# Moving the splits behind a normalisation, and additions, statistics and turns one step on, in a state-space and MLP kernel

## The chip, the core and the metric

The kernel runs on one core of a Trainium2 chip. The metric is device time in microseconds (us) of one execution; before the change it is 699.3 us, the median of three runs (698.97 to 700.25). The core has a matrix engine (TensorE, PE in the profile, with its weight loads as PEld), a vector engine (VectorE, DVE), an activation engine (ScalarE, ACT), a general engine (GpSimd, POOL) and a queue that issues DMAs (SyncE, SP). Each engine works through its own list of instructions strictly in the order written; semaphores join the lists.

## What is computed

Two residual blocks on x of 2048 rows (time) by 512 columns (channels), all in float32:

```python
def _A_ref(u, ...):                       # S4D convolution along time
    K = 2.0 * jnp.einsum("dn,dnl->dl", C, P).real
    y = irfft(rfft(u_t, 2 * L) * rfft(K, 2 * L))[:, :, :L]
    return y + u * D_skip
def _B_ref(x, w1, w2, w3, w4):
    h = _gelu(_layernorm(x) @ w1)
    hs = concat(h shifted by +1, -1, +2, -2 rows, one quarter of the channels each) @ w2
    x1 = x + hs
    return x1 + _gelu(_layernorm(x1) @ w3) @ w4
h  = x + _A_ref(_layernorm(x), ...)
h2 = h + _B_ref(_layernorm(h), w1, w2, w3, w4)
```

w3 is 512 by 1792, w4 is 1792 by 512.

## The kernel before

The convolution (`conv_phase`) takes the first 303 us and is not touched. A planner writes its order; after it, everything in `mixer_phase` runs in the order in which the Python code stands. Whatever one function issues to an engine stands in that engine's list behind what earlier calls issued.

**Tiles and groups.** The 2048 rows of h are 16 tiles of 128 rows, tile j in `h[:, j, :]`; four tiles make a group, so group q holds tiles 4q to 4q+3. Every matrix product is made of three float32r products (high by high, high by low, low by high), so each factor is split into a high half (a rounding copy) and a low half (the difference). Matmuls of the mixer are 128x128 by 128x512.

**Layers 1 and 2.** `layer1(q, f)` makes 12 matmuls and a GELU. `layer2(j)` (line 1265) makes 12 matmuls for tile j into one of four rotating PSUM banks and lets VectorE write x1 of the tile from it; in the profile these blocks are `l`, and their evacuation is `xq<-h,rr,l`. For tiles 0 to 7 it calls at once `residual(j)`, which adds x1 to h (on GpSimd for tiles below 12, on VectorE from 12 on; `h<-h,xq`), and `stats2(j)`, two VectorE instructions for mean and variance (`st`, `mv`).

**The second normalisation.** `norm2_ops(q)` (line 1290) gives, for a whole group, eleven small VectorE steps on 128x4 numbers that work out 1/sqrt(var) and the offset (`qa`, `qb`, `qr`, `qo`), and then four normalisations of 128x512, on ScalarE; of group 1 the last is VectorE's. `norm2(q)` issues all of them at once.

**Turns.** The normalised groups have to be transposed. `turn2(q)` (line 1314) does it with four VectorE block transposes and 16 DMAs within the core's memory, in SP's queue; `turn2_wide(1)` with 16 TensorE transposes into four wide banks (`x1t`), each bank copied out by ScalarE.

**Layer 3 with seven products.** The product with w3 uses Strassen's scheme (in Winograd's form) on pairs of groups: pair 0 is groups 0 and 1, pair 1 groups 2 and 3. Its left factors are the turned blocks b11, b21, b22 and the sums t1 to t4 from `sums2` (four VectorE subtractions for each half c), each split by `halve` (line 1340): the high half on ScalarE, the low half on VectorE, or on GpSimd where told. For pair 0, b11 and b21 (turned group 0) are split on GpSimd (`b1100l` to `b2101l`), before `layer2(7)`.

**The loop of steps** (line 1542) runs s = 0 to 13; steps 0 to 6 work on pair 0, steps 7 to 13 on pair 1. Each step makes, on TensorE: products a, b, c, e of six matmuls each (`l3a` ...; step 0 has the order a, f, e, c, b, d, g); the first half of layer 4 for the step before (`layer4a`, 24 matmuls into the wide banks, `acc`); products f, d, g; and the second half (`layer4b`, four blocks of six matmuls into the rotating banks, `l`). The seven products go through the same four rotating banks. VectorE adds each product from its bank to its sum `u`; each finished sum goes through two GELUs on ScalarE (a rounded one and a full one), and VectorE makes the low half from both. GpSimd makes low halves and sums of the weights (`raws`, `w3s`, `ptw`, `amp0w`, ...). The bank of the second of the four layer-4 blocks is the one that f was in, of the third the one that d was in, of the fourth the one that g was in: TensorE can't start them before VectorE has emptied those.

At step 6 (`turn`), `fresh` splits the factors of pair 1: eight halves before the step's product f is evacuated, six at its end.

**Where the moved work stands before.** `layer2` for tiles 8 to 15 issues neither additions nor statistics; these, the normalisation and the turns of groups 2 and 3 stand by hand in the loop, between `layer4a` and `layer3b`: additions 8 to 11 in step 0, statistics and normalisation of group 2 in step 1 (with additions 12 and 13 at its end), turn of group 2, statistics 12 to 15, additions 14 and 15 and normalisation of group 3 in step 2, turn of group 3 in step 3, subtractions of the sums in steps 4 and 5. `todo` is a list of closures, and `some(n)` issues the next n of it.

Of the kernel before, what the change touches and what calls it, by code (L numbers as in the profile page):

```python
# [1128 lines left out]
def mixer_phase(ctx, tc, cst, h, out, finish, w3, w4):  # L1129
# [15 lines left out]
    def slot(i):  # L1145
        return cst["slab"](i)
# [10 lines left out]
    def bank(name):  # L1157
        return ps.tile([128, 512], F32, tag="bank", name=name)
# [11 lines left out]
    def gelu(b, name):  # L1170

        hi, lo, g = slab(f"{name}h"), slab(f"{name}l"), tmp(f"g{name}")
        nc.scalar.activation(hi, b, AF.Gelu_apprx_tanh)
        nc.scalar.activation(g, b, AF.Gelu_apprx_tanh)
        nc.vector.tensor_tensor(lo, g, hi.bitcast(F32), ALU.subtract)
        return hi, lo
# [50 lines left out]
    def layer1(q, f):  # L1227
        b = bank(f"l1_{q}_{f}")
        n = 0
        seq = [(c, wi, xi) for c in range(4) for wi, xi in PROD]  # L1230
        if (q, f) == (3, 0):

            seq.sort(key=lambda k: 2 * k[0] + 3 * k[2])
        for c, wi, xi in seq:
            nc.tensor.matmul(b, W1[f][wi][:, c * 128 : c * 128 + 128], XT[q][c][xi], start=(n == 0), stop=(n == 11))
            n += 1
        H1[q, f] = gelu(b, f"h1_{q}_{f}")

        tiles = {0: ((15, 0),), 2: ((14, 1), (15, 2)), 1: ((0, 3),), 3: ((0, 4), (1, 5))}[f]
        for t, i in tiles:  # L1240
            if t // 4 != q:
                continue
            for k in range(2):
                src = H1[q, f][k][:, t % 4 * 128 : t % 4 * 128 + 128]
                dst = wrap[k][i // 4][:, i % 4, :]
                if f in (0, 2):
                    nc.gpsimd.tensor_copy(dst[:, 32:128], src[:, 0:96].bitcast(F32))
                    nc.gpsimd.tensor_copy(dst[:, 1:32], src[:, 96:127].bitcast(F32))
                    nc.gpsimd.tensor_copy(dst[:, 0:1], zero)
                else:  # L1250
                    nc.gpsimd.tensor_copy(dst[:, 0:96], src[:, 32:128].bitcast(F32))
                    nc.gpsimd.tensor_copy(dst[:, 96:127], src[:, 1:32].bitcast(F32))
                    nc.gpsimd.tensor_copy(dst[:, 127:128], zero)
# [11 lines left out]
    def layer2(j):  # L1265
        q, i = divmod(j, 4)
        b = bank(f"l2_{j}")
        n = 0
        for f, sh in enumerate((-1, 1, -2, 2)):
            for wi, xi in PROD:  # L1270
                nc.tensor.matmul(b, h1_block(f, j + sh, xi), W2[f][wi], start=(n == 0), stop=(n == 11))
                n += 1
        x1 = quarter(X1[q], i)
        nc.vector.scalar_tensor_tensor(x1, h[:, j, :], r1[:, j : j + 1], b, ALU.mult, ALU.add)
        xq[j] = x1
        if j < 8:
            residual(j), stats2(j)

    def residual(j):
        (nc.gpsimd if j < 12 else nc.vector).tensor_tensor(h[:, j, :], h[:, j, :], xq[j], ALU.add)  # L1280

    def stats2(j):
        q, i = divmod(j, 4)
        if q not in mv2:
            mv2[q] = sm.tile([128, 4, 2], F32, tag="mv2", name=f"mv2_{q}")
        st = sm.tile([128, 6], F32, tag="bst", name=f"st1_{j}")
        nc.vector.bn_stats(st, xq[j])
        nc.vector.bn_aggr(mv2[q][:, i, :], st)

    def norm2_ops(q):  # L1290

        m = mv2[q]
        ra_, rb_, rs = (sm.tile([128, 4], F32, tag=f"q{i}", name=f"q{i}") for i in "abr")
        o = sm.tile([128, 4], F32, tag="qo", name="qo")
        ops = rsqrt_ops(nc, m[:, :, 1], EPS, rs, ra_, rb_)
        ops.append(lambda: nc.vector.scalar_tensor_tensor(o, m[:, :, 0], -1.0, rs, ALU.mult, ALU.mult))
        for i in range(4):
            x1 = xq[q * 4 + i]
            if (q, i) == (1, 3):
                ops.append(lambda: nc.vector.tensor_scalar(x1, x1, rs[:, 3:4], o[:, 3:4], ALU.mult, ALU.add))  # L1300
            else:
                ops.append(lambda i=i, x1=x1: nc.scalar.activation(x1, x1, AF.Identity, scale=rs[:, i : i + 1], bias=o[:, i : i + 1]))
        return ops

    def norm2(q):
        for op in norm2_ops(q):
            op()
# [6 lines left out]
    def turn2(q):  # L1314

        x, t = X1[q], XQ[{0: 2, 2: 3, 3: 1}[q]]
        blocks = t.rearrange("p (b c i t) -> p i c b t", b=4, c=4, i=4)
        for i in range(4):
            nc.vector.transpose(blocks[:, i], quarter(x, i).rearrange("p (c b t) -> p c b t", c=4, b=4))
        for a in range(4):  # L1320
            for b in range(4):
                nc.sync.dma_start(quarter(x, a)[b * 32 : b * 32 + 32], quarter(t, b)[a * 32 : a * 32 + 32])
        for c in range(4):
            FT[q, c] = turned(x)[:, c]

    def turn2_wide(q):

        tiles = [xq[q * 4 + i] for i in range(4)]
        for c in range(4):
            b = wide_bank(c, f"x1t{q}_{c}")  # L1330
            for i, t in enumerate(tiles):
                nc.tensor.transpose(b[:, i * 128 : i * 128 + 128], t[:, c * 128 : c * 128 + 128], ident)
            FT[q, c] = turned(X1[q])[:, c]
            nc.scalar.copy(FT[q, c].rearrange("p a (i t) -> p i a t", i=4), natural(b))
# [26 lines left out]
    todo = []  # L1361

    def some(n):
        while n and todo:
            todo.pop(0)()
            n -= 1
# [12 lines left out]
    def sum3():  # L1379
        a11, a12, a21, a22 = (raw[n][:, i * 256 : i * 256 + 256] for n in "ab" for i in range(2))  # L1380
        s1, s2, s3, s4 = (raw["s"][:, i * 256 : i * 256 + 256] for i in range(4))
        nc.gpsimd.tensor_tensor(s1, a21, a22, ALU.add)
        nc.gpsimd.tensor_tensor(s3, a11, a21, ALU.subtract)
        nc.gpsimd.tensor_tensor(s2, s1, a11, ALU.subtract)
        nc.gpsimd.tensor_tensor(s4, a12, s2, ALU.subtract)
# [16 lines left out]
    def raw4(s):  # L1402
        for i in range(2):
            f = s % half + i * half
            nc.sync.dma_start(raw["45"[i]], w4[f * 128 : f * 128 + 128, :])

    def load4(s):
        W4[s] = []
        for i in range(2):
            o, r = s % 2 * 4 + i * 2, raw["45"[i]]  # L1410
            nc.scalar.copy(slot(o), r)
            nc.gpsimd.tensor_tensor(slot(o + 1), r, slot(o).bitcast(F32), ALU.subtract)
            W4[s].append((slot(o), slot(o + 1)))
# [13 lines left out]
    norm1(2), sum3(), layer1(1, 0), layer1(1, 1), layer1(1, 2), turn1(2), layer1(1, 3), load3(0), raw3(1)  # L1427
    layer2(2), layer2(3), norm2(0), layer2(4), layer2(5)
    layer1(2, 0), turn2(0), layer1(2, 1), load4(0), raw4(1), layer1(2, 2), sum3(), layer1(2, 3), layer2(6)
    for n in ("b11", "b21"):  # L1430
        for c in range(2):
            halve(FT[0, c + 2 * (n == "b21")], 0, n, c, nc.gpsimd)
    layer2(7), norm2(1), layer2(8), layer2(9), layer2(10), turn2_wide(1)
    rest = []
    for c in range(2):
        t1, t3, t2, t4 = sums2(0, c)
# [105 lines left out]
    for s in range(2 * half):  # L1542
        turn, last = s + 1 == half, s + 1 == 2 * half
        layer3a(s)
        if turn:
            fresh(("b11", "t2", "t3", "t1"))
        if last:
            load4(s)
        else:
            load3(s + 1, *((nc.gpsimd,) if s else (nc.vector, range(1, 3))))  # L1550
        if s + 2 < 2 * half:
            raw3(s + 2)
        if s:
            layer4a(s - 1)
        if s == 0:
            for j in range(8, 12):
                residual(j)
        if s == 1:
            for j in range(8, 12):
                stats2(j)  # L1560
            todo.extend(norm2_ops(2)), some(11)
        if s == 2:
            turn2(2)
            for j in range(12, 16):
                if j > 13:
                    residual(j)
                stats2(j)
            todo.extend(norm2_ops(3)), some(11)
        if s == 3:
            turn2(3)  # L1570
        if s == 4 or s == 5:
            todo.extend(sums2(1, s - 4))
            some(4)
        late = layer3b(s)
        if not last and s:
            load4(s), raw4(s + 1)
        if s + 2 < 2 * half:
            sum3()
        if s:
            layer4b(s - 1, late)  # L1580
        else:
            late()
        some(4)
        if s == 1:
            residual(12), residual(13)
        if turn:
            fresh(("b21", "t4", "b22"))
    layer4a(2 * half - 1), layer4b(2 * half - 1, lambda: None)
# [44 lines left out]
```

## Time and profile before

| what | value |
|---|---|
| time, median of 3 runs | 699.3 us (698.97 to 700.25) |
| the profiled execution, own time | 699.71 us |
| its span, first to last instruction | 697.7 us |
| mean granted TensorE clock | 0.993 of full |
| TensorE busy | 658.5 us (94%) |
| VectorE busy | 541.4 us (78%) |
| ScalarE busy | 411.1 us (59%) |
| GpSimd busy | 396.6 us (57%) |
| TensorE busy, first 400 us of the span | 365.12 us |
| TensorE busy, 400 to 680 us | 279.87 us of 280 |

A row of the timeline reads: start and duration in us, engine, line, operation, output<-inputs, partitions x elements and type, count, and in brackets how long the engine was idle before it and who released it. A row of the chain of work that ended last reads: start, duration, engine and output, count. A row of the table by stretches reads: stretch, its length, busy time and (number of instructions) of TensorE, its weight loads, VectorE, ScalarE and GpSimd, then the granted clock, the share of the DMA engines and GB/s. All instructions of both phases carry line 87, that of a helper, so one goes by the names of tiles.

### The profile page before, as it was taken

To read this page: it belongs to the slowest core of one execution; us is meant where nothing else is said; L and a number is where in the kernel's file an instruction comes from. 1 tells how busy PE (TensorE), PEld (TensorE's weight loads), DVE (VectorE), ACT (ScalarE), POOL (GpSimd) and SP (SyncE) were. 2 spreads that over 40 slices of the span, in tenths; PEclk is the share of its full clock that TensorE was granted. 3 is DMA by queue.
4 is the path that set the end of the run, shared out by engine and by line. 5 is a ranking of instruction groups with operands and counts; after the bars stand their busy time and mean duration, and the time that the engine had idled before them with its cause. 6 is when DMAs were issued, how large, how long until landed. Compare 5 with 4: busy or idle time off the path is not lost.

```text
span 697.7 us, 16761 instructions
## 1 busy us (share of the span) xinstructions
PE 658.5 (94%) x6854; PEld 513.8 (74%) x6854; DVE 541.4 (78%) x946; ACT 411.1 (59%) x712; POOL 396.6 (57%) x406
## 2 busy tenths in 40 slices
PE   5987999998999988989999899999999999999997
PEld 5884756653676774858888688888888888888886
DVE  5998898999898998987776789967569954554544
ACT  7888788877899883247643345364445543444330
POOL 1889589877999997002555504655533655553310
PEclk9998999999999999999999999999999999999999
DMA  8830653011201222020013001334111352211004
GB/s 219 261 130 2 199 161 87 2 47 32 64 15 35 62 84 88 2 62 0 1 31 90 1 15 46 91 99 114 46 47 31 96 147 60 61 46 45 16 15 121
DMA packets 47216, 48.34 MB, mean 69 GB/s; under 512 B 5668, under 2 KB 32292, under 8 KB 47140
## 3 DMA queue, kind: packets, MB, share of 16 engines
q1 hardware_dynamic: 46372, 46.22, 23.0%
q10 hardware_dynamic: 768, 1.05, 0.6%
q8 instruction: 54, 0.88, 0.5%
q14 instruction: 22, 0.18, 0.1%
HBM read 35.72 MB, written 8.39 MB: 63 GB/s over the span
## 4 chain that ended last, share of the span: by engine, by line
PE 57%; DVE 18%; ACT 12%; POOL 5%; issue 4%; DMA 2%; SPq 1%; DVEq 0%; ACTq 0%; POOLq 0%
PE l L87 22%; PE acc L87 10%; ACT pt L87 7%; PE bank L87 5%; DVE u L87 4%; PE l3c L87 3%; PE l3e L87 3%; DVE at L87 3%; PE l3b L87 3%; PE l3f L87 3%; PE l3a L87 3%; PE l3g L87 2%; PE l3d L87 2%; DVE sn L87 2%; DVE cs L87 2%
## 5 line engine op out<-in xcount | busy, mean ns | idle before, releaser
L87 ACT ACTIVATE pt<-pt 128x1056 f32<-128x1056 int32 x64 | 69.9, 1092 | 14.6 <-DVE cs L87 6.5
L87 POOL TENSOR_TENSOR pt<-p,s 128x512 int32<-128x512 int32 x64 | 71.5, 1134 | 5.1 <-DVE sn L87 4.1
L87 PE MATMUL bank<-at,tbs 128*64 128x128 f32 (+1 forms) x768 | 63.1, 311 | 3.1 <-DVE u L87 1.4
L87 PEld LDWEIGHTS bank<-at,tbs 128*64 128x64 f32 x768 | 44.6, 134 | 20.3 <-ACT at L87 3.0
L87 PEld LDWEIGHTS bank<-ident 128*128 128x128 f32 x418 | 51.1, 200 | 8.3 <-issue 5.1
L87 PE MATMUL bank<-ident 128*128 128x128 f32 x418 | 55.2, 289 | 0.0
L87 PE MATMUL bank<-u,ms 64*128 64x128 f32 x768 | 50.6, 280 | 3.7 <-DVE u L87 1.5
L87 PEld LDWEIGHTS bank<-u,ms 64*128 64x128 f32 x768 | 45.3, 187 | 8.6 <-DVE u L87 2.3
L87 POOL TENSOR_TENSOR cs0w<-raw,cs0w 128x512 fp32r<-128x512 f32 x7 | 9.4, 1343 | 63.4 <-ACT cs0w L87 63.4
L87 DVE TENSOR_TENSOR h<-h,l 128x512 f32<-128x512 f32 x48 | 32.4, 685 | 13.3 <-PE l L87 13.3
L87 DVE TENSOR_TENSOR cs<-pt,amx 128x512 f32<-128x512 f32 x64 | 40.8, 675 | 2.4 <-ACT pt L87 1.3
L87 DVE TENSOR_TENSOR u<-u,l3f 128x512 f32<-128x512 f32 x14 | 9.6, 684 | 42.6 <-PE l3f L87 42.6
L87 POOL TENSOR_TENSOR cs1w<-raw,cs1w 128x512 fp32r<-128x512 f32 x7 | 9.1, 1297 | 57.2 <-ACT cs1w L87 57.2
L87 PEld LDWEIGHTS bank<-cs 128*32 128x32 f32 x1024 | 24.2, 111 | 22.5 <-POOL cs L87 6.1
L87 PE MATMUL bank<-cs 128*32 128x64 f32 x1024 | 32.6, 225 | 8.5 <-DVE cs L87 4.0
L87 ACT COPY at<-bank 128x512 f32<-128x512 f32 x40 | 24.9, 629 | 23.0 <-PE bank L87 22.9
L87 ACT ACTIVATE pt<-pt,halfpi 128x1056 f32<-128x1056 f32 x32 | 38.1, 1189 | 0.5
L87 POOL TENSOR_TENSOR sn<-pt,amp 128x512 f32<-128x512 f32 x30 | 36.8, 1226 | 1.4 <-ACT pt L87 1.0
L87 DVE STREAM_TRANSPOSE at<-bank 128x512 f32<-128x512 f32 (+1 forms) x40 | 35.5, 916 | 1.9 <-PE bank L87 1.8
L87 ACT ACTIVATE u<-u 128x512 f32<-128x512 f32 x56 | 35.4, 633 | 1.8
L87 PE MATMUL bank<-sn 128*32 128x64 f32 x1024 | 31.9, 222 | 2.5 <-DVE sn L87 2.5
L87 POOL TENSOR_TENSOR cs<-pt,amp 128x512 f32<-128x512 f32 x26 | 31.9, 1228 | 3.5 <-PE bank L87 1.1
(1163 smaller groups left out, 2085.2 us busy)
## 6 DMA issues: line engine op xcount, KB each, us to landing
raw<-in_B_w_dram SPq DMA_DIRECT2D x28, 256.0 KB, 2.7
h<-in_A_u_dram SPq DMA_DIRECT2D x32, 128.0 KB, 4.2
h<-in_A_u_dram SPq DMA_DIRECT2D x16, 256.0 KB, 4.3
rawa<-in_B_w_dram SPq DMA_DIRECT2D x14, 256.0 KB, 2.9
rawb<-in_B_w_dram SPq DMA_DIRECT2D x14, 256.0 KB, 2.8
ms<-in_mm_dram SPq DMA_DIRECT2D x4, 768.0 KB, 10.7
xq<-xq SPq DMA_DIRECT2D x48, 64.0 KB, 2.0
out_dram<-h SPq DMA_DIRECT2D x48, 64.0 KB, 1.7
```

Source lines behind the costliest of these rows:

```text
L87: ins = f(*args, **kw)
```

## The change

It moves calls and changes no computation. First, the splits of b11 and b21 of pair 0 (four high copies on ScalarE, four low halves on GpSimd) are issued behind `layer2(7)` and `norm2(1)` instead of ahead of them. Second, in the loop, the additions of tiles 8 to 11 move from step 0 to step 1, the normalisation of group 2 from step 1 to step 2, the additions of tiles 12 to 15 to step 2 behind that normalisation, the turn of group 2 and the normalisation of group 3 from step 2 to step 3, the turn of group 3 from step 3 to step 4, and the subtractions of the first half of pair 1's sums from step 4 to step 5, where those of the second half are now issued at the step's end.

```diff
     layer1(2, 0), turn2(0), layer1(2, 1), load4(0), raw4(1), layer1(2, 2), sum3(), layer1(2, 3), layer2(6)
+    layer2(7), norm2(1)
     for n in ("b11", "b21"):
         for c in range(2):
             halve(FT[0, c + 2 * (n == "b21")], 0, n, c, nc.gpsimd)
-    layer2(7), norm2(1), layer2(8), layer2(9), layer2(10), turn2_wide(1)
+    layer2(8), layer2(9), layer2(10), turn2_wide(1)
...
-        if s == 0:
-            for j in range(8, 12):
-                residual(j)
         if s == 1:
             for j in range(8, 12):
-                stats2(j)
-            todo.extend(norm2_ops(2)), some(11)
-        if s == 2:
-            turn2(2)
-            for j in range(12, 16):
-                if j > 13:
-                    residual(j)
-                stats2(j)
-            todo.extend(norm2_ops(3)), some(11)
-        if s == 3:
-            turn2(3)
-        if s == 4 or s == 5:
-            todo.extend(sums2(1, s - 4))
-            some(4)
+                residual(j), stats2(j)
+        if s == 2:
+            for j in range(12, 16):
+                stats2(j)
+            norm2(2)
+            for j in range(12, 16):
+                residual(j)
+        if s == 3:
+            turn2(2), norm2(3)
+        if s == 4:
+            turn2(3)
+        if s == 5:
+            todo.extend(sums2(1, 0) + sums2(1, 1)), some(4)
         late = layer3b(s)
...
         some(4)
-        if s == 1:
-            residual(12), residual(13)
```

Before, `some(11)` issued the eleven small steps ahead of `layer3b` and the `some(4)` at the end of the step issued the four normalisations; `norm2` issues both ahead of `layer3b`, so ScalarE gets the normalisations ahead of the step's GELUs. The built lists of instructions show the same: on ScalarE three normalisations stand ahead of the four high copies of b11 and b21; on GpSimd the addition of tile 7 ahead of the four low halves, and the additions of tiles 8 to 11 behind step 1's weight splits; in SP's queue each turn's 16 DMAs behind one more set of weight loads.

## The prediction

> **What bounds the kernel now.** First the page, for the share of each engine.
>
> ```profile
> span 697.7 us, 16761 instructions
> PE 658.5 (94%) x6854; PEld 513.8 (74%) x6854; DVE 541.4 (78%) x946; ACT 411.1 (59%) x712; POOL 396.6 (57%) x406
> L87 ACT ACTIVATE u<-u 128x512 f32<-128x512 f32 x56 | 35.4, 633 | 1.8
> ```
>
> TensorE works for 658.5 of 697.7 us. An edit that adds and removes no matmul can only change the time by making TensorE wait, or no longer wait. So the second view is the chain of work that ended last, near the two edits, and TensorE's timeline where that chain leaves TensorE.
>
> ```profile
> 346.58 1.75 PE xt L87 x16
> 381.57 1.16 DVE qr L87
> 386.50 1.20 DVE qo L87
> 387.79 2.23 ACT xq L87 x3
> 390.07 2.66 PE x1t L87 x14
> 444.13 2.40 DVE xq L87 x4
> 448.12 0.58 DVE h L87
> 473.13 5.44 PE l L87 x24
> ```
>
> ```profile
> 386.37 0.39 PE L87 MATMUL l<-ptw,h_3h 128*128 128x512 f32 x1
> 388.66 0.33 PE L87 MATMUL x1t<-ident,xq 128*128 128x128 f32 x1 [1.90 <-ACT xq L87]
> 396.05 0.39 PE L87 MATMUL l<-sn0w,h_0h 128*128 128x512 f32 x1
> 453.75 0.50 PE L87 MATMUL l<-cs1w,h_101h 128*128 128x512 f32 x1
> 535.78 0.39 PE L87 MATMUL l<-cs1w,h_501l 128*128 128x512 f32 x1
> ```
>
> Layer 2's block 10 issues its last matmul at 386.37; matmuls follow each other at 5.44/24 = 0.227, so TensorE was free at 386.60. The turn of group 1 (`x1t`) starts only at 388.66, after 1.90 of waiting for ScalarE, and its last 14 transposes at 390.07: the first two, of 0.33 each, leave 0.75 of further waiting. Behind it TensorE is also slow:
>
> ```profile
> 303.00:306.00 3.00, 2.02 (x20) 0.85 (x11) 2.63 (x11) 1.89 (x3) 0.00 (x0) 1.00 0.09 25
> 390.10:394.00 3.90, 3.90 (x18) 3.61 (x19) 1.26 (x3) 2.76 (x5) 3.18 (x3) 0.58 0.01 2
> ```
>
> The granted clock (the figure after POOL's count) is 0.58 in 390.1 to 394. Block 12 starts at 396.05. Undisturbed, 16 transposes take 1.75 (the `xt` row) and block 11's 12 matmuls 2.72, so block 12 would start at 386.60 + 1.75 + 2.72 = 391.07. The stretch holds 4.98 us that no matmul needs: 2.66 of waiting and 2.32 of slow clock.
>
> Who is late? VectorE and GpSimd ahead of that wait:
>
> ```profile
> 380.37 0.17 DVE L87 TENSOR_SCALAR qa<-mv 128x4 f32<-128x4 f32 x1
> 381.37 1.33 POOL L87 TENSOR_TENSOR b1100l<-xq,b1100h 128x512 fp32r<-128x512 f32 x1 [3.35 <-ACT b1100h L87]
> 386.41 1.26 POOL L87 TENSOR_TENSOR h<-h,xq 128x512 f32<-128x512 f32 x1
> 380.67 0.62 ACT L87 CAST b1100h<-xq 128x512 fp32r<-128x512 f32 x1 [6.69 <-DMA xq<-xq]
> ```
>
> The eleven small steps of norm2(1) cost 0.2 apiece from 380.37 to 381.57, but the last five, 381.57 to 387.69, take 1.2 each, one per GpSimd operation: the four low halves of the splits (381.37 to 386.41) and an addition to h. VectorE gets its turn only when a GpSimd operation ends. ScalarE's three normalisations (387.79, 2.23) come after the last step, then the turn.
>
> **Part one: the splits behind norm2(1).** ScalarE's order becomes three normalisations, then the four high copies; GpSimd's the additions of tiles 6 and 7, then the four low halves. No low half exists until ScalarE has made the copies, so none can lock the small steps. The addition of tile 7 (1.26) now runs from about 379.5 to 380.75 and delays the first small step from 380.37 to there; ten more at 0.2 end at 382.8, the three normalisations at 385.1. That is before 386.60, with 1.5 to spare: both the waits and the slow clock go, 4.98.
>
> What is late next: the copies, then the sums.
>
> ```profile
> 390.59 1.07 ACT L87 COPY xq<-x1t 128x512 f32<-128x512 f32 x2 [0.58 <-PE x1t L87]
> 389.08 4.20 POOL L87 TENSOR_TENSOR h<-h,xq 128x512 f32<-128x512 f32 x3 [1.41 <-DVE xq L87]
> 391.21 0.93 DVE L87 TENSOR_TENSOR t<-xq,xq 128x512 f32<-128x512 f32 x1 [0.89 <-ACT xq L87]
> 396.25 0.75 DVE L87 SCALAR_TENSOR_TENSOR xq<-h,rr,l 128x512 f32<-128x512 f32 x1 [1.06 <-PE l L87]
> 408.23 0.68 DVE L87 TENSOR_TENSOR xq<-xq,t 128x512 f32<-128x512 f32 x1
> 409.92 0.69 DVE L87 TENSOR_TENSOR u<-u,l3f 128x512 f32<-128x512 f32 x1 [1.01 <-PE l3f L87]
> ```
>
> The four copies to their high halves take 385.1 to 387.2 on ScalarE, the low halves about 385.8 to 391 on GpSimd. The first copy out of the turn lands at about 387.9 instead of 391.2, so VectorE's first subtraction can be asked for 3.2 earlier than 391.21, but now beside the last three low halves, each up to 1.3 of lock. I let them alternate with the first three SBUF operations: block 11's evacuation (396.25 before) ends at 392.2 to 393.4, 3.6 to 4.8 earlier. From there to the last subtraction (408.23) the chain is VectorE's own, without port waits, because the additions of tiles 8 to 11 (389.08, 4.20 for three) are moved out. It ends at 404 to 405 instead of 408.9. Product f's evacuation was due at 409.92 with 1.01 of waiting for TensorE, and is now due at 404.94: met, with 0.1 missing to 0.9 spare. From there VectorE follows TensorE as before, so TensorE keeps the 4.98. Bounds: 4.0 if the lock costs one GpSimd operation more, 5.2 if the waiting of 0.22 at block c of step 1 also goes.
>
> **Part two: one step on.** I keep the old clock here, with everything shifted alike.
>
> ```profile
> 438.24 2.21 DVE L87 TENSOR_TENSOR h<-h,xq 128x512 f32<-128x512 f32 x2
> 450.95 0.18 DVE qa L87
> 453.02 0.68 DVE L87 TENSOR_TENSOR u<-u,l3f 128x512 f32<-128x512 f32 x1
> 443.79 2.41 POOL L87 TENSOR_TENSOR amp0w<-raws,sn1w 128x1024 fp32r<-128x1024 f32 x1
> 470.44 0.69 DVE L87 TENSOR_TENSOR u<-u,l3f 128x512 f32<-128x512 f32 x1 [3.12 <-PE l3f L87]
> 467.31 0.74 POOL L87 TENSOR_TENSOR w3s<-rawb,w3s 128x256 fp32r<-128x256 f32 x1
> 447.39 10.02 SPq L1322 DMA_DIRECT2D xq<-xq  x16
> ```
>
> Step 1 loses eleven small steps (2.2) ahead of its evacuation of f and two additions behind it (438.24: 1.1 each beside GpSimd instead of 0.58). Against that stand GpSimd's four additions (5.2 of lock), now beside the low halves of the activations; alternating costs VectorE some 3, of which 1.5 come off the 2.2 it gained and nothing reaches the banks TensorE wants. 0.
>
> Step 2 loses four turns (2.40) and gains two additions (0.58 each); norm2(2) takes norm2(3)'s place. Statistics alone stand ahead of it, so the small steps start at 450.95 - 2.40 - 1.16 = 447.4 and end at 449.5; four additions later, f is evacuated from 451.9 instead of 453.02, and TensorE's wait at 453.75 (0.22) goes. But ScalarE holds four normalisations (2.23/3 x 4 = 3.0) in front of the first GELU pair (2 x 0.63): GELUs end at 449.5 + 3.0 + 1.3 = 453.8, the low half comes behind them, so the evacuation of d stays at 454.9 and the third l4 block waits 0.1 to 0.2 instead. 0, from -0.2 to +1.
>
> Step 3 takes turn2(2) and norm2(3): turns end where VectorE goes idle now, at 470.44 - 3.12 = 467.3; the small steps wait for GpSimd until 468.05 and end at 470.0, just before f. ScalarE: 470.0 + 3.0 + 1.3 = 474.3; with a low half and an evacuation of 0.68 each, d is out at 475.6. The third l4 block, half of 5.44 behind 473.13, wants it at 475.85. It fits by 0.2; the later blocks too. 0, up to +1 if ScalarE is a microsecond later. The 16 DMAs of each turn (10.02 of SP's queue) move past one pair of weight loads each; those have 20 us to land. 0.
>
> Steps 4 to 6: turn2(3) takes the place of four subtractions; step 5 keeps four subtractions and gets four more at its end.
>
> ```profile
> 522.18 0.69 DVE L87 TENSOR_TENSOR u<-u,l3b 128x512 f32<-128x512 f32 x1 [2.09 <-PE l3b L87]
> 526.05 0.68 DVE L87 TENSOR_TENSOR b1110l<-xq,b1110h 128x512 fp32r<-128x512 f32 x1
> 534.72 0.67 DVE L87 TENSOR_TENSOR u<-u,l3f 128x512 f32<-128x512 f32 x1
> 521.29 0.74 POOL L87 TENSOR_TENSOR raws<-rawa,raws 128x256 f32<-128x256 f32 x1
> 526.11 1.77 POOL L87 TENSOR_TENSOR amp0w<-rawa,sn1w 128x512 fp32r<-128x512 f32 x1 [4.09 <-ACT sn1w L87]
> ```
>
> This is the one place with no slack. In step 6 VectorE makes eight low halves (from 526.05) and then evacuates f until 535.39; the block that wants that bank starts its second matmul at 535.78, 0.03 behind the rhythm. The four subtractions start at 520.09 (522.18 less the 2.09 of idleness) and meet GpSimd's four additions of 0.74 (the last ends at 522.03), so they end at 523.5 to 524.3. The four evacuations that ran from 522.18 to 526.05, with pauses, follow without one and end at 526.1 to 526.75. The copy of the second t2 on ScalarE waits for its subtraction, about 1 us, and with it GpSimd's split at 526.11, which then falls wholly on the low halves (+0.5). The evacuation of f slips by 0.3 to 1.2; TensorE waits for it. +0.8 taken, nearer the late end because each piece is back to back. Such a wait would not slow the clock: at 303 to 306 TensorE is busy 2.02 of 3.00 and the clock stays at 1.00.
>
> **Sum.** -4.98 + 0.8 + 0.1 (steps 2 and 3) = -4.1. The profiled execution took 699.71 (span 697.7 and 2.0 around it), 0.4 over the median of 699.3; the median becomes 695.2.
>
> [...] Here three gaps that add to 2.66 go with a granted clock of 0.58. [...]
>
> **Rivals.**
> (A) All hidden: the late subtractions fit in VectorE's pauses ahead of 526.05 (5.96 from 520.09 less four evacuations: 3.3), and TensorE waits nowhere new. 699.3 - 5.0 = 694.3. For it: the subtractions alone are 2.4. Against: GpSimd's additions lie just there. 0.22.
> (B) The late GELUs count: in steps 2 and 3 ScalarE's head of queue is 1 us later each than I worked out. Two more microseconds: 697.2. For it: margins of 0.2. Against: in step 3 VectorE had 3.12 of waiting ahead of f, which the moved work now fills, not more. 0.14.
> (C) The slow clock is not the gap's doing and stays: -2.66 + 0.8: 697.4. Against: the slow stretch begins where the gap ends, and the shorter gap at 303 to 306 shows 1.00. 0.04. [...]
> (D) Slower: the lock returns to the small steps elsewhere. GpSimd's four additions push its weight splits later in steps 1 and 2, so that the group of 1.3, 2.4 and 0.74 falls on norm2(2), and norm2(3) meets the next one; each step then loses 4.4 at ScalarE's late GELUs: 695.2 + 8.8 = 704.0. It decides when GpSimd's last split of step 2 ends after 447.3 on the old clock; it ended at 443.79 + 2.41 + 0.74 = 446.9, and I expect 446.1 because the two additions on VectorE no longer hold the port. 0.07.
> (E) The first wait is not removed, since something else holds the turn: GpSimd's addition of tile 7 or the copies. Then only +0.8 remains: 700.1. The order of instructions speaks against it: nothing else stands ahead of the three normalisations. 0.03.
> My forecast has the other 0.50.
>
> **Range and chances.** From 693.9 (A with 0.4 more) to 697.6 (B, C and the bounds of part one and step 6); D and E are left out. Changes within 0.2% (1.4 us), about what a measurement of this kernel can tell from none, are E and a thin part of B: 0.05. Slower is D, 0.07. Faster 0.88.
>
> **What would show it.** In the profile after: small steps of norm2(1) at 0.2, ScalarE's normalisations of group 1 near 383, no wait in front of `x1t`, clock 1.0 behind it, block 12 at 391.1, product a of step 0 five earlier. In step 6, at the second l4 block, a new wait of 0.3 to 1.2 on VectorE's `u<-u,l3f`. Waits in front of the third l4 block of steps 2 or 3 would speak for B; small steps of 1 us there for D; a clock under 0.7 near 390 without a gap for C. I am wrong in the main point if block 12 starts later than 392.5.

## The result, and the profile after

The changed kernel takes 694.57 us, the median of six executions (694.29 to 695.73); the kernel before 699.07, also of six (697.4 to 700.25). The ratio is 0.994, with a 95% interval of 0.9926 to 0.9955, so 4.5 us are gained; the prediction said 4.1 (695.2 us). The number alone does not decide for it, since rival A's 694.3 lies nearer; the wait at step 6, below, does. The profiled execution took 695.48 us, 4.23 less than that of before. The page's line of busy times after the change:

```profile
PE 656.0 (95%) x6854; PEld 511.8 (74%) x6854; DVE 538.6 (78%) x946; ACT 411.2 (59%) x712; POOL 397.8 (57%) x406
```

TensorE's busy time fell by 2.5 us with the same 6854 matmuls. 2.15 of it lies at the turn of group 1 and block 11 (6.63 busy from 388.66 to 396.05 before, 4.48 from 386.67 to 391.15 after): the same work at a better clock, and without transposes that go one by one. The chain of work that ended last, first two rows of before, then the rows of after at the same places and those that answer to the prediction's (start, duration, engine and output, count):

```profile
407.10 1.36 PE l3a L87 x6
539.85 1.36 PE l3a L87 x6
```

```profile
386.83 1.75 PE x1t L87 x16
388.58 13.62 PE l L87 x60
402.19 1.36 PE l3a L87 x6
468.08 5.44 PE l L87 x24
535.51 1.37 PE l3a L87 x6
```

The turn of group 1 follows block 10 without a wait, 16 transposes in one row of 1.75. Product a of step 0 starts 4.91 us earlier (402.19 for 407.10), the second half of layer 4 in step 3 is 5.05 earlier (468.08 for 473.13), and product a behind step 6 only 4.34 (535.51 for 539.85). So nearly the whole gain arises at one place, and 0.7 of it is given back at one place. The timeline and the table by stretches show how:

```profile
380.44 0.41 DVE L87 TENSOR_SCALAR qa<-mv 128x4 f32<-128x4 f32 x1
382.66 0.16 DVE L87 SCALAR_TENSOR_TENSOR qo<-mv,qr 128x4 f32<-128x4 f32 x1
382.92 2.23 ACT L87 ACTIVATE xq<-xq,qo,qr 128x512 f32<-128x512 f32 x3 [8.88 <-DVE qo L87]
379.53 1.28 POOL L87 TENSOR_TENSOR h<-h,xq 128x512 f32<-128x512 f32 x1 [1.46 <-DVE xq L87]
385.74 1.30 POOL L87 TENSOR_TENSOR b1100l<-xq,b1100h 128x512 fp32r<-128x512 f32 x1 [4.92 <-ACT b1100h L87]
389.96 1.82 DVE L87 TENSOR_TENSOR t100l<-t,t100h 128x512 fp32r<-128x512 f32 x1 [1.13 <-ACT t100h L87]
405.02 0.69 DVE L87 TENSOR_TENSOR u<-u,l3f 128x512 f32<-128x512 f32 x1 [0.39 <-PE l3f L87]
390.10:394.00 3.90, 3.90 (x19) 3.24 (x18) 3.54 (x4) 0.32 (x1) 1.13 (x1) 1.00 0.00 0
```

The first small step of norm2(1) waits for the addition of tile 7, which ends at 380.81, and is done at 380.85; the other ten take 0.2 each, and the last ends at 382.82 instead of 387.69. ScalarE's three normalisations end at 385.15, ahead of the 386.67 at which TensorE comes free, and the first low half of b11 starts only at 385.74, when there is nothing left of the normalisation to lock. The granted clock in 390.1 to 394 is 1.00; it was 0.58. The lock has moved to the sums (1.82 for a low half of 0.69), where it fits: product f of step 0 is evacuated with 0.39 to spare.

In steps 2 and 3, and then in 5 and 6:

```profile
439.96 0.76 POOL L87 TENSOR_TENSOR sn0w<-rawb,sn0w 128x256 fp32r<-128x256 f32 x1
442.35 0.14 DVE L87 TENSOR_SCALAR qa<-mv 128x4 f32<-128x4 f32 x1
444.31 0.16 DVE L87 SCALAR_TENSOR_TENSOR qo<-mv,qr 128x4 f32<-128x4 f32 x1
450.00 0.50 PE L87 MATMUL l<-cs1w,h_101h 128*128 128x512 f32 x1
517.08 1.95 DVE L87 TENSOR_TENSOR xq<-xq,xq 128x512 f32<-128x512 f32 x2
518.96 0.68 DVE L87 TENSOR_TENSOR u<-u,l3b 128x512 f32<-128x512 f32 x1
530.37 0.67 DVE L87 TENSOR_TENSOR u<-u,l3f 128x512 f32<-128x512 f32 x1
531.10 0.50 PE L87 MATMUL l<-cs1w,h_501h 128*128 128x512 f32 x1 [0.46 <-DVE u L87]
```

The small steps of norm2(2) run from 442.35 to 444.47 at 0.2 each, behind GpSimd's last weight split (ends 440.72). The four subtractions end at 519.03 and the evacuation of l3b follows them without the 2.09 us of idleness it had before. Eight low halves later f is evacuated at 530.37, and TensorE's second block waits for it at 531.10: the new wait.

### The profile page after: what moved, and what is told of

It reads as the page before. It is cut to its first block, busy times and chain, and to the rows that moved or that the text cites. A ratio compares the mean times of both kernels' runs of the same rounds, so it can differ in the third digit from the quotient of the medians.

```text
span 693.4 us, 16766 instructions
## 1 busy us (share of the span) xinstructions
PE 656.0 (95%) x6854; PEld 511.8 (74%) x6854; DVE 538.6 (78%) x946; ACT 411.2 (59%) x712; POOL 397.8 (57%) x406
## 4 chain that ended last, share of the span: by engine, by line
PE 58%; DVE 19%; ACT 12%; issue 4%; POOL 4%; DMA 2%; SPq 1%; DVEq 0%; ACTq 0%; POOLq 0%
PE l L87 24%; PE acc L87 10%; ACT pt L87 7%; PE bank L87 6%; DVE u L87 5%; DVE at L87 3%; DVE cs L87 3%; DVE sn L87 3%; PE l3c L87 3%; PE l3f L87 3%; PE l3e L87 3%; PE l3a L87 2%; PE l3b L87 2%; PE l3g L87 2%; PE l3d L87 2%
```

## The experiments

All times below are medians; the kernel before took 699.38 us on the chip of the experiments 1, 2, 3 and the first of 6, and 699.78 on that of the others. Gains and losses against it are worked out from the ratio, which has its 95% interval. The theory: the gain is the lock of GpSimd's low halves on VectorE's small steps taken away, with the slow clock behind it, and 0.6 to 0.7 is lost in step 6. The rivals: the first edit brings all of it alone; the slow clock is not the wait's doing; the step 6 loss is something else.

**1. The first edit alone** (the loop as before):

```diff
+    layer2(7), norm2(1)
     for n in ("b11", "b21"):
...
-    layer2(7), norm2(1), layer2(8), ...
+    layer2(8), ...
```

> Only the first edit: the splits of b11 and b21 behind norm2(1); the loop as before. My theory: the 5.0 us at the turn of group 1 go, as in the changed kernel, but the additions of tiles 8 to 11, still issued in step 0, now follow the low halves on GpSimd without a pause (391 to 399) and lock four of VectorE's operations on the sums, 1.2 to 1.3 each; the evacuation of product f of step 0 comes some 3 us after TensorE could use it. Net -2.0 (-1.4 to -3.0): 697.1 against 699.1. Rival, that the first edit carries the whole gain alone: -5.0, 694.1, with f's evacuation waiting for TensorE.

Measured 697.1 us; ratio 0.9969 (0.9958 to 0.9981), 2.2 less than before. The timeline of this run:

```profile
392.42 6.84 POOL L87 TENSOR_TENSOR h<-h,xq 128x512 f32<-128x512 f32 x4
398.03 1.78 DVE L87 TENSOR_TENSOR t300l<-xq,t300h 128x512 fp32r<-128x512 f32 x1
407.09 0.47 PE L87 MATMUL l3e<-t100h,ptw 128*128 128x512 f32 x1 [0.94 <-ACT t400h L87]
413.16 0.47 PE L87 MATMUL l3g<-b2200h,ptw 128*128 128x512 f32 x1 [0.38 <-DVE u L87]
```

GpSimd's four additions of tiles 8 to 11 (6.84 from 392.42) lie beside the subtractions and low halves of the sums, which take 1.0 to 1.8 instead of 0.69. The chain comes out late, and TensorE waits for factors and evacuations: 0.94 and 0.38 in front of products e and g, and 0.25 in front of c of step 1, which starts 0.44 behind the rhythm of the matmuls (0.22 before). Product a of step 1 starts 11.35 after that of step 0 (403.27, 414.62), where it is 9.52 before and after the change: step 0 loses 1.83 here. By the medians 2.2 of the 4.5 come without the loop's change, as expected, and the rival that the first edit is enough falls.

**2. The loop's change alone** (the splits ahead of the normalisation, as before; everything else of the change):

> Only the second edit: additions, statistics and turns one step on; the splits ahead of norm2(1) as before. My theory: the turn of group 1 waits as before (2.7 and the slow clock), and step 6 adds its wait of 0.6 at the second layer-4 block: +0.5 (+0.2 to +1.0), 699.6. Rival, that the moved work shortens steps 0 to 3 by itself: -0.5 or better.

Measured 700.46 us; ratio 1.0011 (1.0002 to 1.002), 0.8 more than before. A row of its timeline and two of its chain:

```profile
387.61 0.33 PE L87 MATMUL x1t<-ident,xq 128*128 128x128 f32 x1 [1.89 <-ACT xq L87]
533.98 0.61 DVE u L87
534.63 4.40 PE l L87 x18
```

The wait at the turn is there (1.89, then 0.38 and 0.26), and so is the late second block of step 6 (18 matmuls from 534.63, behind f, which is evacuated until 534.59). Alone this half of the change only costs. The two halves add up to 2.2 - 0.8 = 1.4, and together they bring 4.2 to 4.5: moving the additions off step 0 pays some 3 us by the medians, whose intervals leave more than 1 us of that open, but only once the splits are behind the normalisation and the sums are what is late. What the profiles show of it is the 1.83 of step 0.

**3. The first edit and the additions of tiles 8 to 11 in step 1**, with the normalisation of group 2 still there and all that follows as before:

```diff
-        if s == 0:
-            for j in range(8, 12):
-                residual(j)
         if s == 1:
             for j in range(8, 12):
-                stats2(j)
+                residual(j), stats2(j)
             todo.extend(norm2_ops(2)), some(11)
```

> The first edit, and of the second only the additions of tiles 8 to 11 from step 0 to step 1; the normalisations and turns stay in their steps. My theory: the 5.0 us go and step 6 has no new wait, but the four additions on GpSimd now run beside the eleven small steps of norm2(2) in step 1 and lock them, four times 1.25: the evacuation of f of step 1 comes 4 to 5 us late and TensorE waits some 3 us at the second layer-4 block of step 1. Net -2.0 (-1.2 to -3.2), 697.1. Rival, that the lock matters only near the turn of group 1: -5.0, 694.1.

Measured 698.68 us; ratio 0.9989 (0.998 to 0.9998), only 0.8 less than before: the direction was right, but the gain lies outside the range given (1.2 to 3.2), and the loss is larger than forecast. The timeline of step 1 and the stretches round the wait:

```profile
423.59 5.01 POOL L87 TENSOR_TENSOR h<-h,xq 128x512 f32<-128x512 f32 x4
423.68 1.22 DVE L87 TENSOR_SCALAR qb<-qa 128x4 int32<-128x4 int32 x1
427.42 1.20 DVE L87 SCALAR_TENSOR_TENSOR qb<-qb,qa 128x4 f32<-128x4 f32 x1
430.45 0.50 PE L87 MATMUL l<-cs0w,h_001h 128*128 128x512 f32 x1 [2.54 <-DVE u L87]
427.45:430.86 3.41, 0.87 (x5) 0.40 (x4) 3.21 (x9) 0.43 (x1) 1.14 (x1) 1.00 0.00 0
430.86:434.27 3.41, 3.41 (x10) 2.64 (x9) 3.25 (x6) 3.16 (x6) 0.00 (x0) 0.50 0.00 0
```

The turn is without a wait here, too (block 11 starts at 387.80), but the four additions now lock four small steps of norm2(2) (1.2 each, 423.68 to 428.62). The steps stand ahead of the evacuation of f, TensorE waits 2.54 for it, and 0.4 later the clock falls to 0.50 for 3.41 us. From product a of step 1 to that of step 2 pass 25.21 us (20.75 before): 4.46 lost, where the expectation had counted the wait and no slow clock. It is the fault of the kernel before, at another place.

**4. The same without those four additions:**

```diff
-                residual(j), stats2(j)
+                stats2(j)
```

> The run with the splits and the additions once more, with the additions of tiles 8 to 11 to h left out (so h of these tiles lacks them). Theory: what that run lost against the changed kernel, about 4 us, is GpSimd's 5.01 us of additions beside the small steps of the third group's normalisation (four steps of 1.22 instead of 0.2), which made product f late, TensorE wait 2.54 and the clock fall; without the additions the steps take 0.2 each, no wait and no slow clock are left in step 1, and the time is 694.2 us (693.8 to 695.0), 5.1 below the kernel before. Rival: with the work of step 0 ending 5 us earlier the eleven small steps ahead of f are late in step 1 in any case, or the loss lies in steps 2 to 6: then it stays within 1 us of that run, 698 to 699.

Measured 695.01 us; ratio 0.9937 (0.9923 to 0.995), 4.4 less than before, at the upper edge of what was expected. The timeline and the chain:

```profile
424.23 0.17 DVE L87 TENSOR_SCALAR qb<-qa 128x4 int32<-128x4 int32 x1
427.04 5.44 PE l L87 x24
```

The steps take 0.2, the blocks of layer 4 run through in 5.44, and step 1 takes 20.75 again. The loss of the run before was the lock on four of the eleven tiny instructions, with the slow clock behind it, and nothing in steps 2 to 6. This is why the change has to move the normalisation of group 2 together with the additions: it is the additions' way out, not a gain of its own.

**5. Three of the four splits ahead again** (from the changed kernel; `split(n, c)` is one call of `halve` with its low half on GpSimd):

```diff
+    split("b11", 0), split("b11", 1), split("b21", 0)
     layer2(7), norm2(1)
-    for n in ("b11", "b21"): ...
+    split("b21", 1)
```

> The changed kernel with three of the four splits (both of b11, the first of b21) back ahead of the second group's normalisation and one behind it. Before, five GpSimd operations (four low halves and the addition of tile 7) locked five small steps, the last from 386.50 to 387.69; with one low half fewer four are locked, the last small step ends near 386.6, the first normalisation near 387.4, and the turn waits 0.8 us and then some 0.5 to 0.75 in two pieces: about 1.5 us of waiting in place of none after and 2.66 before. Theory: the granted clock falls only behind a long stretch without matmuls (2.66 us of waiting in 3.5 us before, 2.54 in one piece in the run with the splits and the additions), and 1.5 us is not one; then the clock stays at 1.00 and the time is the changed kernel's plus 1.5: 696.1 us (695.6 to 696.6), 3.3 below the kernel before. Rival: any wait over about a microsecond that holds the turn brings the slow clock (0.5 to 0.6 for four microseconds), then 2 us more: 698.1, 1.2 below the kernel before.

Measured 698.32 us; ratio 0.9982 (0.9972 to 0.9992). The changed kernel beside it took 695.05, so three low halves cost 3.3 us, a difference that the two intervals leave uncertain by about 1.1. Its timeline and stretches:

```profile
382.99 1.14 DVE L87 SCALAR_TENSOR_TENSOR qr<-qb,qr 128x4 f32<-128x4 f32 x1
386.59 1.29 POOL L87 TENSOR_TENSOR h<-h,xq 128x512 f32<-128x512 f32 x1
387.80 0.39 PE L87 MATMUL l<-ptw,h_3h 128*128 128x512 f32 x1
389.06 0.33 PE L87 MATMUL x1t<-ident,xq 128*128 128x128 f32 x1 [0.87 <-ACT xq L87]
390.46 1.75 PE L87 MATMUL x1t<-ident,xq 128*128 128x128 f32 x14 [0.38 <-ACT xq L87]
391.97 0.47 PE L87 MATMUL l<-sn0w,h_0h 128*128 128x512 f32 x1
388.00:391.41 3.41, 1.79 (x12) 1.23 (x12) 2.61 (x5) 3.15 (x5) 0.41 (x1) 1.00 0.00 0
391.41:394.82 3.41, 3.41 (x21) 2.90 (x19) 2.43 (x3) 2.15 (x5) 0.86 (x1) 1.00 0.02 7
```

Four steps are locked (382.99 to 387.90), one per GpSimd operation, as foretold. The waits read 0.87, 0.38 and 0.38, the clock stays at 1.00, and that is the theory's side. But the time lies at the rival's 698.1. Some 2.3 of the 3.3 can be read: from block 10's last matmul (387.80, 0.227 to the next start) to block 11's first (391.97) pass 3.94 us; after the change it was 386.44 to 388.33, that is 1.66. I had added up the waits alone, 1.5; two transposes that go one by one take 0.70 from start to start each, where back to back they are 0.10 apart (1.66 for 16). The last microsecond stays open. The one profiled execution (699.22) was 1.4 later than that of the changed kernel already in front of the turn, at a place that the edit does not touch; the stretches below show a slow clock there. The mean clock of the twelve executions is 0.992 in the median, that of the changed kernel beside them 0.995 in five of six. One stretch of 3.41 us at half the clock makes 0.0024 of that (1.71 of 697), so most of the others, too, had about one such stretch more; where it lay is not shown.

The clock itself: the stretches ahead of and behind the point where it falls, in the kernel before and in the run with the loop's change alone.

```profile
387.32:390.73 3.41, 1.32 (x8) 0.94 (x9) 2.89 (x5) 2.36 (x4) 2.00 (x3) 1.00 0.00 0
390.73:394.14 3.41, 3.41 (x14) 3.12 (x13) 1.18 (x2) 2.63 (x5) 2.55 (x2) 0.50 0.03 7
```

```profile
384.98:388.39 3.41, 1.14 (x6) 0.49 (x4) 3.27 (x5) 1.65 (x3) 1.65 (x2) 1.00 0.00 0
388.39:391.80 3.41, 3.15 (x14) 2.86 (x15) 1.58 (x3) 2.09 (x4) 0.00 (x0) 0.50 0.01 2
```

Three times (these two and experiment 3) the clock is 0.50 for 3.41 us and then 1.00 again, and in the 3.41 us ahead of it TensorE was busy for 1.32, 1.14 and 0.87. These stretches lie on a fixed grid: in the kernel before the clock comes back at 66.46 and falls at 390.73, 95 times 3.413 us later (the length of the piece that begins there). Where the grid cuts a wait matters. The run of experiment 5 shows it, three stretches of its own grid, and then the changed kernel's stretch at the place of the first, where the two kernels do the same:

```profile
258.87:262.28 3.41, 1.37 (x82) 0.95 (x66) 3.41 (x6) 3.38 (x8) 3.33 (x4) 1.00 0.21 61
262.28:265.69 3.41, 3.41 (x32) 3.41 (x32) 2.92 (x5) 0.89 (x2) 3.41 (x5) 0.50 0.29 99
388.58:391.99 3.41, 2.18 (x17) 1.81 (x17) 2.52 (x5) 3.33 (x7) 0.99 (x1) 1.00 0.01 2
```

```profile
259.91:263.32 3.41, 2.09 (x82) 1.93 (x72) 3.41 (x7) 3.01 (x7) 3.41 (x5) 1.00 0.44 154
```

The grid lies a microsecond apart in the two executions. So the same pauses leave TensorE busy for 1.37 of one stretch in the run of experiment 5, and the clock falls behind it; in the changed kernel they leave 2.09, and it stays. At the turn of experiment 5 the stretch of the grid is busy for 2.18. Three windows of 3.41 us around that wait, from 387.60, 388.00 and 388.20, are busy for 1.79, 1.79 and 1.80. In the profiles of before and after, from 15 us to the last matmul, the clock fell from 1.00 behind the stretches of the grid that were busy for 0.70 (56.22 to 59.64, before), for 1.17 (55.11 to 58.52, after) and for the 1.32 above, and behind no other; the least busy of the others had 1.83 (28.91 to 32.33, before) and 2.04 (27.80 to 31.21, after). So a wait near 2.5 us costs itself and, where the grid leaves a stretch as little busy as those behind which the clock fell (0.70 to 1.37), up to 1.7 more; that is an estimate, half of 3.41. The waits that brought it at the turn and in step 1 were of 2.5 to 2.7 us in all, in stretches that were not idle (1.32, 1.14 and 0.87 busy).

**6. The eight subtractions together in step 5, ahead of the step's evacuations** (from the changed kernel), run twice, the second time beside the changed kernel:

```diff
-            todo.extend(sums2(1, 0) + sums2(1, 1)), some(4)
+            todo.extend(sums2(1, 0) + sums2(1, 1)), some(8)
```

> The changed kernel with one number changed: all eight subtractions of pair 1's sums ahead of layer3b of step 5, none at its end. My theory of step 6: VectorE idles 2.7 us ahead of f of step 5, which takes the four moved ones; the eight low halves of step 6 start on time and the new wait of 0.46 in front of the second layer-4 block goes. -0.6 against the changed kernel (-0.3 to -0.8), 694.0, -5.1 against before. Rival, that the wait of step 6 comes from the turn moved to step 4 or from GpSimd's splits: no change against the changed kernel.

> The changed kernel with the eight subtractions issued together ahead of step 5's evacuations, once more, beside the changed kernel on the same chip. Its profile of the first run has no wait at the second block of step 6. Theory: 0.6 below the changed kernel, 694.0. Rival: the wait has only been taken over by something that a single profile does not show, and the two are the same within 0.2.

> The changed kernel unaltered, on one chip with the next. Theory: 694.6 us, 4.7 below the kernel before, with 0.62 lost in step 6 at the second block's wait for f.

Measured 694.26 us, ratio 0.9937 (0.9924 to 0.9951), and then 694.77, ratio 0.9931 (0.9918 to 0.9944); the changed kernel again 695.05, ratio 0.9935 (0.9923 to 0.9947). Rows of the first run's timeline, then of the chains of the second run and of the changed kernel beside it:

```profile
516.63 0.69 DVE L87 TENSOR_TENSOR u<-u,l3b 128x512 f32<-128x512 f32 x1 [2.09 <-PE l3b L87]
529.16 0.67 DVE L87 TENSOR_TENSOR u<-u,l3f 128x512 f32<-128x512 f32 x1
529.97 0.42 PE L87 MATMUL l<-cs1w,h_501h 128*128 128x512 f32 x1
```

```profile
529.67 5.49 PE l L87 x24
```

```profile
531.16 4.40 PE l L87 x18
```

With the subtractions out of VectorE's pause, l3b is met after 2.09 us of idleness again, f is evacuated at 529.16, in time, and the second block starts within 0.03 of the rhythm. In the second run the four blocks are one piece of 5.49; in the changed kernel the chain leaves TensorE and comes back for the last 18 matmuls. From product a of step 0 to product a behind step 6 pass 132.6 us in both of these runs and 133.3 in both of the changed kernel: the profiles show the wait gone, and 0.7 us with it. The medians are 0.3 lower both times, once on one chip; the intervals overlap, so it is the best version here in the profile, but its time is not told from that of the changed kernel. The second run's profile also has a stretch at half the clock from 261.52 to 264.94, far ahead of the edit, which the changed kernel's lacks (mean clock 0.992, there 0.995); one such stretch costs more than the 0.7 (up to 1.7).

## Why the prediction came out

**What bounded the kernel.** Right: a lock of one small step per GpSimd operation held the turn. The forecast of its removal was exact to 0.1: small steps to end at 382.8 (382.82), normalisations at 385.1 (385.15), first subtraction at 387.9 (387.98), block 11's evacuation done between 392.2 and 393.4 (393.03), last subtraction done between 404 and 405 (404.63), f with 0.1 missing to 0.9 spare (0.39 spare). Of the 4.98, 4.97 came, counted from block 10's last matmul (9.68 to block 12 before, 4.71 after). Block 12 starts at 391.15; the point at which I would have been wrong was 392.5.

**The slow clock.** The prediction took it as the gap's doing, and it went with the gap; rival C, which would have kept it, falls. The split of the 4.98 was off, though: 2.66 of waiting and 2.32 of slow clock. The clock was at 0.50 for 3.41 us, which costs 1.7. The other 0.6 are the transposes that went one by one, whose rows of 0.33 I had counted as work; experiment 5, with such transposes and no slow clock, shows it. The sum was right because both went together.

**One step on.** Step 2 came as worked out: small steps 442.4 to 444.5 (442.35 to 444.47), and a delay of some 0.1 at the third block (450.00, a row of 0.50 where its neighbours have 0.39) in place of the 0.22 at the second. Step 3 gave no wait; rival B falls. Steps 1 to 3 together came to a gain of 0.15 (4.91 to 5.05) where I had put a loss of 0.1. Mis-sized, without effect: in step 1 I reckoned that the additions would cost VectorE some 3 us; its four low halves beside them took 1.0 to 1.2 instead of 0.69, some 1.8.

**Step 6.** Put at 0.8 (0.3 to 1.2), measured at 0.7; f slips by 0.63 (530.37 against 534.72 less 4.98), and the place, the bank and VectorE's late evacuation are those named. The late start of the low halves makes all of the slip (521.74 against 526.05 less 4.98, 0.67). The 0.5 more that the prediction put on GpSimd's split did not come: the eight low halves take 8.63 in all, and took 8.67. Experiment 6 takes it away by undoing the one cause named, the subtractions in VectorE's pause. Rival A needed that loss to be hidden; it was not.

**Rival D** (the lock on the small steps elsewhere) did not come: it was to decide when the last split of step 2 ended after 447.3 on the old clock, 442.3 on the new; it ended at 440.72. The port that the prediction speaks of is in no trace; what they show is that two of GpSimd's operations on `raws` took 1.18 each beside VectorE's additions before (from 438.72) and 0.73 and 0.74 without them after (from 433.44). Experiment 3 shows that the mechanism was real and priced about right at 4.4 for one such step: it cost 4.46 in step 1, though by TensorE's wait for f and the slow clock, not by late GELUs.

**What the prediction did not say** is that its parts do not add. It noted in passing that the sums run free "because the additions of tiles 8 to 11 are moved out"; experiments 1 and 2 show that this half sentence carries some 3 of the more than 4 us by the medians, of which the profiles show 1.83.

## What to carry to other kernels

When a chain of tiny VectorE steps decides when TensorE goes on, look at what GpSimd does in those microseconds: here each of its operations of 1.3 us held one tiny step, for 1.2 instead of 0.2, and an operation that is only moved looks for the next such chain. Follow a freed chain to the next engine that locks it before you count the gain; here an edit worth 2.2 us and one worth less than nothing were worth more than 4 together. Price a wait of TensorE by the distance of its matmuls and by how busy the stretches of 3.41 us around it are left, not by the wait column alone: here the clock fell to 0.50 behind stretches that were busy for 0.70 to 1.37.

## What the runs showed of the hardware

Steps on 128x4 numbers took 1.2 us beside GpSimd operations of 1.3 us, and 0.2 alone. In experiment 3 the statistics just ahead of the locked steps, which read one tile, kept their 0.66 beside GpSimd's weight split of 2.41. The sums (1.82 for 0.69) and the small steps with two inputs (1.20 for 0.2) were held. The small step `qb<-qa` has one tile as input and was locked all the same (1.22 for 0.17), so the number of inputs does not tell what is held; what does, no trace shows. The slow clock came in pieces of 3.41 us, or of twice that (59.64 to 66.46 in the kernel before). Where it fell, TensorE had been busy for 0.70 to 1.37 of the 3.41 us of the grid ahead of it (0.70 and 1.32 before, 1.17 after, 1.14, 0.87 and 1.37 in experiments 2, 3 and 5); in the profiles of before and after it stayed at 1.00 behind every stretch that was busy for 1.83 or more.
